# A fused attention and feed-forward kernel on one core: the first weight load ahead of a conversion, two M1 chunks begun in halves, the first M2 part among the M1 chunks

## The chip, the core and the metric

The kernel runs on one core of a Trainium2 chip. The metric is device time in microseconds (us) of one execution. TensorE is called PE, its weight loads PEld, VectorE DVE, ScalarE ACT, GpSimd POOL, and SyncE SP; L577 is line 577 of the kernel before.

## The reference, cut to what matters

Causal attention with a decay per head, then a feed-forward layer on the attention's output. Batch 8, 8 heads, 576 positions, head size 64; so 4608 tokens of 512 numbers, and a hidden layer of 2048.

```python
log_f = np.log(np.clip(f, 0.0001, 1.0));  cum = np.cumsum(log_f, axis=-1)
scores = scale * (q @ k^T) + cum[..., :, None] - cum[..., None, :]   # causal
attn = softmax(scores);  x = attn @ v          # x is then (4608, 512)
h = x @ w_in                                   # "M1" below
out = (h * sigmoid(h)) @ w_out                 # "M2" below
```

## The kernel before, in words

Everything is in bf16 on PE. The order of the instructions on every engine is written out by hand: each engine executes its own list in order, and an instruction waits for the results, buffers or transfers it needs. So a wait on one engine holds everything behind it there.

The tokens are cut into groups g. The first three groups hold the first 128 positions of each batch: g = 0 has batches 0 to 3 (512 columns), g = 1 batches 4 and 5, g = 2 batches 6 and 7 (256 columns each). The rest of each batch comes later, in a loop over 16 pairs of heads.

For the first 128 positions of batch b the steps are `turn0` (L294, PE turns q and k; ACT and DVE copy them out), `scores0` (L328, and the exponential on ACT, L335), for batches 4 to 7 `mask0` (L344, DVE), `out0` (L368, PE; L377 and L383 on DVE), and `back0` (L398, PE turns the output; L399 copies it into x). `convert_v0` (L349) is a POOL instruction that weights v; `out0` needs it.

M1 is cut into chunks (g, fc), 16 chunks to a group. A chunk is four PE matmuls into a PSUM tile `hp` (L577), a tanh on ACT (`th`, L585), and one DVE instruction that makes `gt` (L586) and frees `hp`. M2 works on 128 tokens at a time in four parts of four matmuls each (L622) into one PSUM tile `po`; after the fourth, ACT copies it to `osb` (L632) and SP stores it (L601). There are four `osb` buffers, so the fifth copy waits until the first store has landed. `hp`, `po` and the tiles of `turn0` and `back0` share a PSUM pool of four tiles.

`fill(us)` puts M1 chunks and M2 parts into the list until so many microseconds of PE work are placed; `step(kind)` puts in one of them, kind 1 being an M1 chunk and kind 2 an M2 part; `ready` is the set of groups whose x is there; M2 is first allowed where `open2["w"]` is set. `two_more(b)` handles batches b and b + 1 (b = 4, then 6) with fills in between. `goal` and `spent()` place the later work by the amount of PE work already in the list.

w_in is loaded in four quarters (`load_w_in`, L199) and w_out in four quarters (L203), by transfers that POOL issues and that cast on the way. Chunks fc = 0 to 3 need the first quarter of w_in. POOL also issues the first loads of q, k and v (L132, L141); SP issues the later ones, after it has seen the second quarter of w_out land (`after`, L209). POOL casts the later q and k (L410, L414), SP turns them by a transposing transfer (L437), and PE scores them (L469). Attention on the later positions ends in `attend` (L516 and L525 on PE, L533 and L534 on DVE), and `back` turns the result (L558).

Of the kernel before, what the change touches and what calls it, by code (L numbers as in the profile page):

```python
# [10 lines left out]
FP32 = mybir.dt.float32  # L11
BF16 = mybir.dt.bfloat16
P = 128
# [5 lines left out]
def kernel(  # L19
# [13 lines left out]
    DM, DFF = moe_w_in.shape  # L33
# [29 lines left out]
    tpool = ctx.enter_context(tc.tile_pool(name="tpool", bufs=3))  # L63
# [36 lines left out]
    def xg(g):  # L100
        if g not in xgs:
            tag, bufs = {4 * P: ("x4", 1), 2 * P: ("x2" if g < 3 else "xt", 2), RB: ("x3", 3)}[GW[g]]
            xgs[g] = xpool.tile([P, NCC, GW[g]], BF16, name=tag, tag=tag, bufs=bufs)
        return xgs[g]

    def xcols(g, cc):

        if g == 3 + NM or g == NG - 1:
            x = xg(g)[:, :, :].rearrange("p (u i) t -> p u (i t)", i=2)[:, cc // 2, :]
            return x.rearrange("p (b i s) -> p i b s", i=2, s=ST)[:, cc % 2, :, :]  # L110
        return xg(g)[:, cc, :]
# [85 lines left out]
    def load_w_in(i):  # L197
        c0, c1 = i * DFF // WQ, (i + 1) * DFF // WQ
        nc.gpsimd.dma_start(out=w_in_bf[:, :, c0:c1], in_=w_in_v[:, :, c0:c1])  # L199
# [106 lines left out]
    def ban0(b):  # L306
        sc = psc.tile([P, 2, NP, P], FP32, name="sc", tag="sc")
        for i in range(2):
            nc.tensor.matmul(  # L309
                sc[:, i, :, :].rearrange("p a t -> p (a t)"),  # L310
                lhsT=ident_bf[:, :],
                rhs=ban[:, :, :].rearrange("p a t -> p (a t)"),
                start=True,
                stop=False,
            )
        return sc

    def scores0(b, sc=None):
        t = qT0.pop(b)
        fresh = sc is None  # L320
        u = upool.tile([P, 2, NP, P], BF16, name="u", tag="u")
        u0[b] = u
        if fresh:
            sc = psc.tile([P, 2, NP, P], FP32, name="sc", tag="sc")
        for p in range(NP):
            for i in range(2):
                r = slice(i * D, (i + 1) * D)
                nc.tensor.matmul(  # L328
                    sc[:, i, p, :],
                    lhsT=kT0[b][r, p, :],  # L330
                    rhs=t[r, p, :],
                    start=fresh,
                    stop=fresh or p == NP - 1,
                )
        nc.scalar.activation(  # L335
            out=u[:, :, :, :].rearrange("p i a t -> p (i a t)"),
            in_=sc[:, :, :, :].rearrange("p i a t -> p (i a t)"),
            func=ACT.Exp,
            scale=scale,
        )  # L340
# [7 lines left out]
    def convert_v0(b):  # L348
        nc.gpsimd.tensor_tensor(  # L349
            out=v0[b][:, :, :],  # L350
            in0=vf0.pop(b)[:, :, :],
            in1=w_bf[:, 0, b * H : (b + 1) * H, None].to_broadcast([P, H, D + 1]),
            op=ALU.mult,
        )
# [36 lines left out]
    def back0(b, *copies):  # L391
        xq = xqs.pop(b)[:, :, :].rearrange("p (c j) d -> p c (j d)", j=2)
        g, c0 = HEADS_OF[b]
        k = NCC // len(copies)
        for n, copy in enumerate(copies):
            tx = pbig.tile([P, k, P], BF16, name="tx", tag="big")
            for cc in range(k):
                nc.tensor.transpose(tx[:, cc, :], xq[:, n * k + cc, :], ident_bf[:, :])  # L398
            copy(out=xg(g)[:, n * k : (n + 1) * k, c0 : c0 + P], in_=tx[:, :, :])  # L399
# [167 lines left out]

    gts: dict[int, bass.AP] = {}

    def m1_chunk(g, fc):  # L570
        w = GW[g]
        if fc == 0:
            gts[g] = gpools[g % 3].tile([P, NFC, w], BF16, name="gt", tag=f"gt{g % 3}")
        gt = gts[g]
        hp = pbig.tile([P, w], FP32, name="hp", tag="big")
        for cc in range(NCC):
            nc.tensor.matmul(  # L577
                hp[:, :],
                lhsT=w_in_bf[:, cc, fc * P : (fc + 1) * P],
                rhs=xcols(g, cc),  # L580
                start=(cc == 0),
                stop=(cc == NCC - 1),
            )
        th = tpool.tile([P, w], BF16, name="th", tag="th")
        nc.scalar.activation(out=th[:, :], in_=hp[:, :], func=ACT.Tanh, scale=0.5)  # L585
        nc.vector.scalar_tensor_tensor(  # L586
            out=gt[:, fc, :],
            in0=th[:, :],
            scalar=1.0,
            in1=hp[:, :],  # L590
            op0=ALU.add,
            op1=ALU.mult,
        )
# [88 lines left out]
    at = {"m1": 0, "m2": 0, "left": 0.0}  # L682
# [23 lines left out]
    def step(force=0):  # L706

        a, c = at["m1"], at["m2"]
        want = wanted(a, c)
        if not want:  # L710
            return None
        g1 = M1[a][0] if a < len(M1) else NG
        g2 = M2[c][0] if c < len(M2) else NG
        can1 = g1 in ready and not (M1[a][1] == 0 and g1 > g2 + lag["g"])
        can2 = open2["w"] and c < len(M2) and g2 < g1
        kind = force if (force == 1 and can1) or (force == 2 and can2) else want
        if kind == 1:
            if M1[a][1] == 0:
                begin[g1] = (0, c)
            m1_chunk(g1, M1[a][1])  # L720
            at["m1"] += 1
            t = 4 * (GW[g1] / 2.4 + 2.5)
        else:
            m2_part(*M2[c])
            at["m2"] += 1
            t = 4 * (DM / 2.4 + 2.5)
        return t

    def behind():
        t = sum(4 * (GW[g] / 2.4 + 2.5) for g, _ in M1[at["m1"] :] if g in ready)  # L730
        t += sum(4 * (DM / 2.4 + 2.5) for g, _, _ in M2[at["m2"] :] if g in ready)
        return t / 1000

    def plan(us_):

        a, c, kinds = at["m1"], at["m2"], []
        while us_ > 0:
            k = wanted(a, c)
            if not k:
                break  # L740
            kinds.append(k)
            if k == 1 and M1[a][1] == 0:
                begin[M1[a][0]] = (0, c)
            us_ -= (4 * (GW[M1[a][0]] / 2.4 + 2.5) if k == 1 else 4 * (DM / 2.4 + 2.5)) / 1000
            a, c = a + (k == 1), c + (k == 2)
        return kinds

    def fill(us_, least=0, ends=(0, 0)):

        left = us_ + at["left"]  # L750
        kinds = plan(left)
        kinds += [0] * (least - len(kinds))
        if any(ends) and kinds:
            if 2 not in kinds:
                kinds[0] = 2
            n1, n2 = len(kinds) - kinds.count(2), kinds.count(2)
            e0 = 1 if ends[0] else 0
            e1 = 1 if ends[1] and n2 > e0 else 0
            inner = n2 - e0 - e1
            n = n1 + inner  # L760
            mid = [2 if (x + 1) * inner // n > x * inner // n else 1 for x in range(n)]
            if inner and mid[-1] == 2 and e1 and not e0:
                mid = mid[::-1]
            kinds = [2] * e0 + mid + [2] * e1
        for k in kinds:
            t = step(k)
            if t is None:
                at["left"] = 0.0
                return
            left -= t / 1000  # L770
        at["left"] = left
# [13 lines left out]
    gpool = ctx.enter_context(tc.tile_pool(name="gpool", bufs=1))  # L785
    first_pool = tc.tile_pool(name="first", bufs=1)
    gpools = [first_pool.__enter__(), gpool, gpool]
    convert_v0(0)
    load_w_in(0)
    turn0(1, 0)  # L790
    turn0(1, 1)
    turn0(2, 0)
# [3 lines left out]
    out0(0, apart=True)  # L796
    turn0(3, 0)
    scores0(2, ban0(2))
    convert_v0(2)
    load_w_in(1)  # L800
    turn0(3, 1)
    bans = ban0(3)
    out0(1, apart=True)
# [10 lines left out]
    back0(1, on_act)  # L814
    out0(3, 1)
    back0(2, on_act)
    back0(3, on_act, on_dve)
    ready.add(0)
    nc.gpsimd.memset(trit[0:ST, :], 0.0)
    make_upper_triangular(nc, trit[ST:P, :], val=1.0, diag=True)  # L820
# [36 lines left out]
    def two_more(b):  # L857
        for x in range(2):
            turn0(b + x, 0)
            turn0(b + x, 1)  # L860
        fill(1.2, 2)
        for x in range(2):
            scores0(b + x)
            mask0(b + x)
        fill(2.6 if b == 4 else 3.4, 3)
        out0(b)
        fill(0.6, 1)
        out0(b + 1)
        fill(0.8, 2)
        back0(b, on_act)  # L870
        fill(0.6, 1)
        back0(b + 1, on_act)
        fill(0.6, 1)

    fill(5.9)
    two_more(4)
    ready.add(1)
    fill(3.0)
    open2["w"] = True
    begin[M1[at["m1"]][0]] = (M1[at["m1"]][1], at["m2"])  # L880
    fill(6.0)
    two_more(6)
    ready.add(2)
    fill(4.2)
# [43 lines left out]
    QUAD = [10.9] * (NQ // 2) + [11.7] * (NQ // 2)  # L928

    def spent():  # L930
        t = sum(4 * (GW[g] / 2.4 + 2.5) for g, _ in M1[: at["m1"]])
        return (t + at["m2"] * 4 * (DM / 2.4 + 2.5)) / 1000

    def rest(target):
# [124 lines left out]
```

## Time and profile before

| what | value |
|---|---|
| median of 3 runs | 340.43 us (340.33 to 341.62) |
| the profiled execution: its own time | 340.98 us |
| the profiled execution: span, first to last instruction | 339.2 us |
| PE busy | 330.6 us, 97% |
| ACT busy | 216.9 us, 64% |
| DVE busy | 193.6 us, 57% |
| POOL busy | 137.4 us, 41% |
| granted TensorE clock | 1.0 |

The span is read as a timeline of queues. Busy shares are averages, so what a change in one stretch is worth is read from that stretch: which engine had idle time in it, and what it waited for. A timeline line gives the start, the length, the engine, the line of the kernel, the output and inputs, the count of merged instructions, and in brackets the idle time before it with what ended it. An issue line gives the time from the issue of a transfer to its landing.

### The profile page before, as it was taken

Reading aid. Unit: us, or ns where it says so; the run is one execution under the profiler, and the core shown is the slowest. Engines: PE = TensorE matmul, PEld = TensorE weight load, DVE = VectorE, ACT = ScalarE, POOL = GpSimd, SP = SyncE. Lnnn points to the kernel's source line nnn. Section 1 sums busy time; section 2 is a strip of 40 time slices with the busy share of each in tenths; the row PEclk is TensorE's granted clock in tenths of the full one; section 3 lists DMA queues with packets and bytes.
Section 4 is the critical chain, followed back from the end, with each engine's and each line's share of the span. In section 5 each row is a group of like instructions: output and inputs, shape, how many; then the busy total and the mean of one; then the engine's idle time right before and its main releaser. Section 6 shows DMA issues by size and latency. Waiting matters only on the chain.

```text
span 339.2 us, 10025 instructions
## 1 busy us (share of the span) xinstructions
PE 330.6 (97%) x4132; PEld 222.4 (66%) x4132; DVE 193.6 (57%) x425; ACT 216.9 (64%) x389; POOL 137.4 (41%) x217
## 2 busy tenths in 40 slices
PE   7999899999999999999999999999999999999995
PEld 3745565577656768857766896867776676555654
DVE  4668935267567556655656865684672558334330
ACT  5766635677867767848748784875776485444431
POOL 8895417636756455454374434536060000000000
PEclk9999999999999999999999999999999999999999
DMA  8999999999999799999998969989763210001012
GB/s 151 190 185 222 182 210 155 199 236 177 156 190 236 117 215 134 163 211 151 168 178 172 142 130 175 134 168 165 148 123 66 56 37 33 31 33 64 33 62 63
DMA packets 144702, 48.00 MB, mean 142 GB/s; under 512 B 133328, under 2 KB 139728, under 8 KB 144656
## 3 DMA queue, kind: packets, MB, share of 16 engines
q1 hardware_dynamic: 115088, 36.60, 59.5%
q0 software_dynamic: 29408, 10.62, 26.6%
q8 instruction: 32, 0.52, 0.7%
q10 hardware_dynamic: 160, 0.13, 0.2%
q14 instruction: 14, 0.11, 0.1%
HBM read 36.85 MB, written 9.44 MB: 136 GB/s over the span
## 4 chain that ended last, share of the span: by engine, by line
PE 92%; ACT 2%; DVE 2%; DMA 2%; issue 1%; POOL 0%; POOLq 0%
PE hp L577 35%; PE po L622 24%; PE pr L648 12%; PE sc L469 7%; PE dn L516 6%; PE dn L525 3%; PE tp L294 2%; DMA qkb<-in_k_dram 2%; DVE u L344 1%; DVE gt L586 1%; ACT x L399 1%; PE sc L309 1%; PE sc L328 1%; ACT u L335 1%; PE tx L558 0%
## 5 line engine op out<-in xcount | busy, mean ns | idle before, releaser
L585 ACT ACTIVATE th<-hp 128x384 bf16<-128x384 f32 (+2 forms) x208 | 96.0, 469 | 78.7 <-PE hp L577 75.8
L586 DVE SCALAR_TENSOR_TENSOR gt<-th,hp 128x384 bf16<-128x384 bf16 (+2 forms) x208 | 107.1, 522 | 67.3 <-ACT th L585 58.5
L577 PE MATMUL hp<-x,w_in_bf 128*128 128x384 bf16 (+2 forms) x704 | 122.1, 321 | 1.5 <-ACT x L399 0.9
L577 PEld LDWEIGHTS <-w_in_bf 128*128 128x128 bf16 x832 | 79.4, 98 | 50.6 <-issue 1.8
L622 PE MATMUL po<-w_out_bf,gt 128*128 128x512 bf16 (+1 forms) x400 | 93.8, 371 | 0.0
L480 ACT ACTIVATE u<-sc 128x1024 bf16<-128x1024 f32 (+1 forms) x96 | 74.4, 814 | 6.4 <-PE sc L469 6.4
L622 PEld LDWEIGHTS <-gt 128*128 128x128 bf16 x400 | 37.6, 98 | 32.5 <-issue 0.2
L410 POOL CAST qkb<-qf 128x384 bf16<-128x384 f32 x32 | 16.7, 522 | 95.1 <-DMA qf<-in_q_dram 94.8
L648 PE MATMUL pr<-w_out_bf,gt 64*128 64x256 bf16 x768 | 46.0, 269 | 0.0
L158 POOL DMA_DIRECT2D qkb<-in_k_dram x56 | 43.8, 784 | 0.7 <-issue 0.7
L648 PEld LDWEIGHTS <-gt 64*128 64x128 bf16 x768 | 38.5, 94 | 2.8
L423 POOL TENSOR_TENSOR vp<-vf,w_bf 128x520 bf16<-128x520 f32 (+1 forms) x32 | 34.1, 1069 | 10.3 <-DMA vf<-in_v_dram 9.0
L632 ACT ACTIVATE osb<-po 128x512 f32<-128x512 f32 (+1 forms) x25 | 14.6, 583 | 22.6 <-PE po L622 19.5
L469 PE MATMUL sc<-qkT 64*128 64x128 bf16 (+1 forms) x640 | 27.9, 206 | 0.4 <-ACT u L480 0.3
L469 PEld LDWEIGHTS <-qkT 64*128 64x128 bf16 x640 | 19.9, 94 | 8.6 <-issue 6.5
L486 DVE TENSOR_TENSOR u<-u,tri 128x768 bf16<-128x768 bf16 x32 | 19.4, 605 | 10.5 <-ACT u L480 10.5
L474 ACT ACTIVATE ut<-sc 128x640 bf16<-128x640 f32 x32 | 22.5, 702 | 1.7 <-PE sc L469 1.3
L516 PEld LDWEIGHTS <-u 128*128 128x128 bf16 x576 | 20.6, 98 | 2.9
L516 PE MATMUL dn<-vp,u 128*128 128x65 bf16 x384 | 21.8, 194 | 0.0
L534 DVE TENSOR_TENSOR xr<-dn,rec 128x448 bf16<-128x448 f32 x32 | 20.0, 624 | 1.1
L516 PE MATMUL dn<-v,u 128*128 128x65 bf16 x192 | 20.0, 194 | 0.0
L577 PE MATMUL hp<-xt,w_in_bf 128*128 128x256 bf16 x128 | 16.6, 273 | 0.0
(72 smaller groups left out, 228.1 us busy)
## 6 DMA issues: line engine op xcount, KB each, us to landing
out_dram<-osb SPq DMA_DIRECT2D x32, 256.0 KB, 3.5
vf<-in_v_dram SPq DMA_DIRECT2D x26, 256.0 KB, 5.5
qf<-in_q_dram SPq DMA_DIRECT2D x64, 96.0 KB, 3.4
qkb<-in_k_dram POOLq DMA_DIRECT2D x56, 48.0 KB, 4.6
w_in_bf<-in_moe_w_in_dram POOLq DMA_DIRECT2D x4, 512.0 KB, 6.8
w_out_bf<-in_moe_w_out_dram POOLq DMA_DIRECT2D x4, 512.0 KB, 8.7
vf<-in_v_dram POOLq DMA_DIRECT2D x6, 256.0 KB, 10.3
qkb<-in_q_dram POOLq DMA_DIRECT2D x8, 128.0 KB, 5.5
```

Of the source, the lines that this page charges most:

```text
L158: nc.gpsimd.dma_start(out=t2[:, NR + 1 : NX, j * D : (j + 1) * D], in_=k[b, head(p, j), P:SM, :].rearrange("(c p) d -> p c d", p=P),)
L423: nc.gpsimd.tensor_tensor(out=vbf[b][r, c, :, :], in0=vst[b][c][r, :, :], in1=w_bf[r, c + 1, b * H : (b + 1) * H, None].to_broadcast([n, H ...
L469: nc.tensor.matmul(sc[:, i, o : o + q1 - q0], lhsT=kt, rhs=t[r, q0:q1], start=True, stop=True)
L474: nc.scalar.activation(out=ut[:, :, 0:3:2, :].rearrange("p k i t -> p i k t"), in_=sc[:, :, T0 : T0 + (NM + 1) * ST].rearrange("p i (k t) ...
L480: nc.scalar.activation(out=u[:, :, c * SM : c * SM + w], in_=sc[:, :, 0:w], func=ACT.Exp, scale=scale)
L516: nc.tensor.matmul(dn[:, i * NR + c - 1, :], lhsT=u[:, i, o : o + P], rhs=vals(kb, i), start=(kb == 0), stop=(kb == c),)
L534: nc.vector.tensor_tensor(out=xq[:, :, p % 2, :], in0=dn[:, :, 0:D], in1=rec[:, :, None].to_broadcast([P, NGR, D]), op=ALU.mult,)
L577: nc.tensor.matmul(hp[:, :], lhsT=w_in_bf[:, cc, fc * P : (fc + 1) * P], rhs=xcols(g, cc), start=(cc == 0), stop=(cc == NCC - 1),)
L585: nc.scalar.activation(out=th[:, :], in_=hp[:, :], func=ACT.Tanh, scale=0.5)
L586: nc.vector.scalar_tensor_tensor(out=gt[:, fc, :], in0=th[:, :], scalar=1.0, in1=hp[:, :], op0=ALU.add, op1=ALU.mult,)
L622: nc.tensor.matmul(po[:, :], lhsT=gt[:, fc, tb * P : (tb + 1) * P], rhs=w_out_bf[:, fc, m0:m1], start=(fc == 0), stop=(fc == NFC - 1),)
L648: nc.tensor.matmul(pos[g, tb][y], lhsT=gt[r, fc, tb * P : (tb + 1) * P], rhs=w_out_bf[r, fc, y * DM // 2 : (y + 1) * DM // 2], start=(half ...
```

## The change

Three things are moved, and the amount of arithmetic stays the same.

1. On POOL's list the load of the first quarter of w_in stands ahead of `convert_v0(0)` instead of behind it, and that of the second quarter ahead of `convert_v0(2)`.
2. Chunks (0, 0) and (0, 1) are each cut into two halves of 256 columns. The halves for batches 0 and 1 are put on PE's list around the last `back0`, one before it and one after it, and their tanh and DVE instructions behind it. The other halves come where the whole chunks were.
3. At the end of `two_more(4)` an M2 part stands in place of a `fill` that found nothing to place, and the M1 chunks of g = 1 that follow are mixed with M2 parts from the start instead of seven chunks ahead of the first part.

By the lists of the two kernels, PE has eight matmuls more (840 of L577 instead of 832), ACT two more tanh and DVE two more `gt` instructions. Some M1 chunks and M2 parts change places up to the fourth of the 16 blocks of the loop; from its attention on, PE's list is the same.

```diff
+    EARLY = 2
+    def cols(g, fc):
+        return slice(2 * P if g == 0 and fc < EARLY else 0, GW[g])
+    def m1_cost(g, fc):
+        r = cols(g, fc)
+        return 4 * ((r.stop - r.start) / 2.4 + 2.5)
     def m1_chunk(g, fc):
+        m1_gate(*m1_mm(g, fc, cols(g, fc)))
+    def m1_mm(g, fc, r):
...
-        hp = pbig.tile([P, w], FP32, name="hp", tag="big")
+        hp = pbig.tile([P, r.stop - r.start], FP32, name="hp", tag="big")
...
-                rhs=xcols(g, cc),
+                rhs=xcols(g, cc) if whole_ else xg(g)[:, cc, r],
...
+    def m1_gate(g, fc, r, hp):
...
+    load_w_in(0)
     convert_v0(0)
-    load_w_in(0)
...
+    load_w_in(1)
     convert_v0(2)
-    load_w_in(1)
...
     back0(2, on_act)
+    first = [m1_mm(0, 0, slice(0, 2 * P))]
     back0(3, on_act, on_dve)
+    first.append(m1_mm(0, 1, slice(0, 2 * P)))
+    for x in first:
+        m1_gate(*x)
...
         back0(b + 1, on_act)
-        fill(0.6, 1)
-
-    fill(5.9)
+        if b == 4:
+            open2["w"] = True
+            step(2)
+        else:
+            fill(0.6, 1)
+
+    fill(5.0)
     two_more(4)
     ready.add(1)
-    fill(3.0)
-    open2["w"] = True
+    for kind in (1, 1, 2, 1, 1, 2, 1, 1, 1, 2):
+        assert step(kind) is not None
+    at["left"] = 0.0
     begin[M1[at["m1"]][0]] = (M1[at["m1"]][1], at["m2"])
-    fill(6.0)
+    fill(2.6)
     two_more(6)
```

More of the change, by code (lines that the diff above doesn't have):

```diff
@@ L568 @@
     gts: dict[int, bass.AP] = {}
+    EARLY = 2
[4 more added lines that the diff above has]
+        return 4 * ((r.stop - r.start) / 2.4 + 2.5)
     def m1_chunk(g, fc):
+        m1_gate(*m1_mm(g, fc, cols(g, fc)))
+    def m1_mm(g, fc, r):
         w = GW[g]
-        if fc == 0:
+        if g not in gts:
             gts[g] = gpools[g % 3].tile([P, NFC, w], BF16, name="gt", tag=f"gt{g % 3}")
-        gt = gts[g]
-        hp = pbig.tile([P, w], FP32, name="hp", tag="big")
+        hp = pbig.tile([P, r.stop - r.start], FP32, name="hp", tag="big")
+        whole_ = r.start == 0 and r.stop == w
         for cc in range(NCC):
@@ L583, in m1_chunk @@
             )
-        th = tpool.tile([P, w], BF16, name="th", tag="th")
+        return g, fc, r, hp
+    def m1_gate(g, fc, r, hp):
+        th = tpool.tile([P, r.stop - r.start], BF16, name="th", tag="th")
         nc.scalar.activation(out=th[:, :], in_=hp[:, :], func=ACT.Tanh, scale=0.5)
         nc.vector.scalar_tensor_tensor(
-            out=gt[:, fc, :],
+            out=gts[g][:, fc, r],
             in0=th[:, :],
@@ L721, in step @@
             at["m1"] += 1
-            t = 4 * (GW[g1] / 2.4 + 2.5)
+            t = m1_cost(*M1[a])
         else:
@@ L729, in behind @@
     def behind():
-        t = sum(4 * (GW[g] / 2.4 + 2.5) for g, _ in M1[at["m1"] :] if g in ready)
+        t = sum(m1_cost(g, fc) for g, fc in M1[at["m1"] :] if g in ready)
         t += sum(4 * (DM / 2.4 + 2.5) for g, _, _ in M2[at["m2"] :] if g in ready)
@@ L743, in plan @@
                 begin[M1[a][0]] = (0, c)
-            us_ -= (4 * (GW[M1[a][0]] / 2.4 + 2.5) if k == 1 else 4 * (DM / 2.4 + 2.5)) / 1000
+            us_ -= (m1_cost(*M1[a]) if k == 1 else 4 * (DM / 2.4 + 2.5)) / 1000
             a, c = a + (k == 1), c + (k == 2)
@@ L930, in spent @@
     def spent():
-        t = sum(4 * (GW[g] / 2.4 + 2.5) for g, _ in M1[: at["m1"]])
+        t = sum(m1_cost(g, fc) for g, fc in M1[: at["m1"]])
         return (t + at["m2"] * 4 * (DM / 2.4 + 2.5)) / 1000
```

## The prediction

> **What bounds the kernel now.** I read the page first, then busy time by stretch.
>
> ```profile
> span 339.2 us, 10025 instructions
> PE 330.6 (97%) x4132; PEld 222.4 (66%) x4132; DVE 193.6 (57%) x425; ACT 216.9 (64%) x389; POOL 137.4 (41%) x217
> ...
> PE 92%; ACT 2%; DVE 2%; DMA 2%; issue 1%; POOL 0%; POOLq 0%
> ```
>
> PE carries 92% of the chain that ended last, so only PE's idle time can be won.
>
> ```profile
> 18.40:38.00 19.60, 18.34 (x168) 9.18 (x168) 15.68 (x24) 12.87 (x23) 15.19 (x25) 1.00 1.18 199
> 38.00:48.00 10.00, 9.58 (x64) 6.15 (x63) 5.02 (x12) 4.68 (x12) 0.00 (x0) 1.00 1.19 205
> 48.00:64.00 16.00, 16.00 (x184) 9.95 (x184) 7.30 (x14) 8.20 (x16) 10.73 (x15) 1.00 1.16 178
> 64.00:85.00 21.00, 20.75 (x308) 14.40 (x307) 12.79 (x33) 16.88 (x32) 11.57 (x19) 1.00 1.30 201
> ```
>
> The columns are the stretch, its length, the busy time of PE, PEld, DVE, ACT and POOL, the clock, the DMA share, GB/s. From 38.4 to 310 us PE is idle for well under 1 us in all. So whatever PE is ahead by when the mixed M1 and M2 work starts stays to the end, unless it meets a new wait. The tail after 310 us is left as it is. PE's timeline shows the idle time before that point:
>
> ```profile
> 17.72 0.61 PE L398 MATMUL tx<-ident_bf,xq 128*128 128x128 bf16 x4 [0.30 <-DVE xq L383]
> 18.46 6.20 PE L577 MATMUL hp<-x,w_in_bf 128*128 128x512 bf16 x28
> ...
> 36.23 1.02 PE L577 MATMUL hp<-x,w_in_bf 128*128 128x512 bf16 x4 [0.19 <-DVE gt L586]
> 37.09 0.39 PE L398 MATMUL tx<-ident_bf,xq 128*128 128x128 bf16 x4
> 38.42 3.22 PE L577 MATMUL hp<-x,w_in_bf 128*128 128x256 bf16 x28 [0.94 <-ACT x L399]
> ```
>
> PE waits around 18 us for the attention of batch 3 and its copies, then in small pieces from 33 us for DVE, then 0.94 us for the copy of batch 5. DVE is late there because its two masks collide with POOL's conversions (the next two lines, from the timelines of DVE and POOL):
>
> ```profile
> 29.99 2.96 DVE L344 TENSOR_TENSOR u<-u,tri 128x1024 bf16<-128x1024 bf16 x2 [0.22 <-ACT u L335]
> 29.89 2.51 POOL L349 TENSOR_TENSOR v<-vf,w_bf 128x520 bf16<-128x520 f32 x2 [4.04 <-DMA vf<-in_v_dram]
> ```
>
> At 52.86 us the same two masks take 1.85 us.
>
> **The early halves.** The half of chunk (0, 0) needs the copies of batches 0 and 1; ACT ends the second at 17.44. PE's turn of batch 2 is out at 17.4, so the half starts at 17.49. The matmul spacing from the rows: (6.20 - 0.38)/27 = 0.216 us for 512 columns, (3.22 - 0.27)/27 = 0.109 us for 256. So the half takes 0.44 us, to 17.92. Batch 3's turn follows at 17.92 to 18.19 (before 17.72 to 18.28 with its waits), the second half at 18.19 to 18.62; its `hp` tile waits for ACT's copy of batch 2, at 18.04. ACT's last copy ends 0.2 us later, at 18.61; the other halves run 18.66 to 19.53; five whole chunks of 0.863 us end at 23.85. Before, seven chunks from 18.46 ended at 24.51: PE is 0.66 us earlier. Eight pairs of 256 columns instead of eight of 512 cost 8 x (0.218 - 0.216), nothing. Two more tanh (0.38 us each) and `gt` (0.42 us) cost nothing: ACT idles 0.27 us before each tanh here and DVE 0.17 us before each `gt`. If that cover fails, `hp` tiles come free late and up to 0.66 us is lost. Bounds: 0 to 0.75.
>
> The Trainium skill ("TensorE: Matmul & The Clock Gate", "Back-to-back issue gap") speaks against the split: it gives a sustained 81 ns per matmul of 128 columns and 131 ns of 512, so by an estimate between them a pair of 256 would cost some 65 ns more than one of 512, 0.5 us over eight pairs. By that rule the gain at the end would be some 0.6 us instead of the sum below. The spacings of 216 and 109 ns in this trace do not agree with it, and I keep the trace's.
>
> **The loads.** w_in's first quarter landed 5.7 us after its issue at 11.28, at 17.0, in time for 17.49 even unmoved. On POOL the load fits between the end of the v issues (9.38) and `convert_v0(0)` (10.28, which waits for the weights), so no conversion moves by over 0.1 us, and `convert_v0(3)` still waits for its v (issued 8.45, landed about 14.7). What moves is the transfers:
>
> ```profile
> 11.00:12.00 1.00, 1.00 (x35) 0.80 (x30) 0.80 (x2) 0.70 (x2) 1.00 (x2) 1.00 1.17 282
> 12.00:13.00 1.00, 1.00 (x25) 0.67 (x21) 0.93 (x5) 1.00 (x2) 0.98 (x2) 1.00 0.61 126
> 13.00:14.00 1.00, 1.00 (x26) 0.65 (x24) 0.34 (x1) 0.77 (x2) 1.00 (x2) 1.00 0.73 65
> 14.00:15.00 1.00, 1.00 (x18) 0.56 (x12) 0.74 (x2) 0.71 (x1) 0.98 (x3) 1.00 1.23 204
> ```
>
> The DMA share is 1.2 when full, and 0.61 and 0.73 from 12 to 14 us: 0.9 us of idle transfer time, which w_in, issued 1.9 us earlier, fills. Later landings queue behind it (10.2 us from issue for v of batch 4), so all come some 1.0 us earlier, between 0 and 1.5.
>
> **DVE's chain to the first chunk of g = 1.** Exponentials come 0.66 us earlier with PE (29.3 and 30.2), and the conversions of batches 4 and 5 about 1.0 us earlier (28.9 and 29.9). In the trace each mask ended 0.55 us after the conversion it met. So the masks end at about 30.5 and 31.95 instead of 32.95: 1.0 us earlier, between 0.65 (PE's lead alone) and 1.45 (no collision, 0.92 us each). The rest is DVE's list as before: three `gt`, the output of batch 4 (34.6), `gt`, output of batch 5 (36.0). PE turns batch 5 at 36.1, ACT copies it by 37.4 instead of 38.38.
>
> **The M2 part.** The wait for that copy is now covered by four matmuls of L622 (0.86 us). Their PSUM tile is that of chunk (0, 13), freed by DVE behind the output of batch 5, at 36.62, so they run 36.67 to 37.53 and the first chunk of g = 1 starts at 37.53, 0.89 us earlier than 38.42 with 0.86 us more done: 1.75 us ahead (bounds 1.4 to 2.2). w_out's quarters landed at 33.3, 35.9, 38.4 and 41.5, even unmoved before the four parts of the first tile are due (36.7, 38.4, 40.1 and 42.3, from 0.86 us a part and 0.44 a chunk). The tile that `po` holds leaves three for the chunks; the order puts at most three between parts.
>
> **Where part of it is given back.** PE's list has the fifth finished M2 tile further ahead: before, its last part and an M1 chunk stood behind both attentions of the first block; now they stand ahead of them. Its copy to `osb` waits for the first store to land, and in the new list the tile of the second attention waits for that copy. ACT and SP before:
>
> ```profile
> 73.19 0.60 ACT L632 ACTIVATE osb<-po 128x512 f32<-128x512 f32 x1 [0.48 <-PE po L622]
> 66.70 2.38 SPq L601 DMA_DIRECT2D out_dram<-osb  x4
> out_dram<-osb SPq DMA_DIRECT2D x1, 256.0 KB, 3.4
> ```
>
> The first store landed at 66.70 + 3.4 = 70.1, 3 us before it was needed. Now ACT reaches the copy at about 69.0. SP's list there follows POOL casts and transfers, so it moves with the transfers: landing at 69.1, copy to 69.75. PE starts the first attention at 69.98 - 1.75 + 0.88 (work moved ahead of it) = 69.1, the second at 70.06 with no wait. But ACT's next two tanh, two `gt` and then both attentions' outputs follow on DVE: `gt` to 70.8, output 1 to 71.6, output 2 to 72.45, and PE, with only 0.55 us of scores between, waits 0.9 us to turn it at 72.5. Before, with the same work done, it did so at 73.63. PE is then 1.1 us ahead: 0.6 us are given back, because nothing stands any more between the second attention and its turn. Bounds: 1.5 ahead with no wait at ACT, 0.1 ahead if the store lands unmoved at 70.1.
>
> Later waits have cover: the transposed q and k of block 2's second pair landed 1.7 us before use, before, and PE's list has 0.9 us more ahead of it now; the others landed over 5 us early.
>
> **Sum.** 1.75 - 0.6 = 1.1 us. The profiled execution would go from 340.98 to 339.9; the median of the runs shown is 0.55 below it, so I predict 340.43 - 1.1 = 339.3.
>
> **Rivals.**
>
> *All of it passes.* The store lands well before ACT needs it (the transfers gain 1.5 us), DVE follows at once, the masks collide less: 1.6 to 2.3 us ahead, about 338.5. For it: transfers are saturated up to 110 us. Against: the output chain of DVE alone takes 1.1 us, with 0.55 us of PE work over it. Chance 0.22.
>
> *Nothing is left.* The transfers do not move, since w_in only waits behind v of batch 3, which landed at 14.7 anyway. Then the store lands at 70.1 and PE turns at 73.55: 340.3, between 339.9 and 340.7. Chance 0.15.
>
> *Slower through the first store.* SP's loads now begin while the last w_out quarters still flow, and the store meets a full queue. A v load between 81 and 90 us took 6.8 us to land; the median of v loads is 5.5. A store of 5.5 us instead of 3.4, issued at 65.7 to 66.7, lands at 71.2 to 72.2; ACT stands still with the exponentials behind it, and the turn is at 74.6 to 75.6: 1.0 to 2.0 us slower than before, about 341.8. It decides where the store lands after 70.2; each later microsecond costs one. Chance 0.16, a good third of it beyond 0.5%.
>
> *The halves do not start early* (an `hp` tile or the w_in quarter late): 0.66 us less at 24 us, but DVE's collision and the M2 part stay, so 0.5 us ahead, 339.9. It lies in the forecast's own range.
>
> **Numbers.** The forecast (0.5 to 1.6 us ahead, 338.8 to 339.9) has 0.47. 0.5% is 1.7 us, about what a measurement of this kernel can tell from no change. Faster by more: most of the first rival, 0.2. Slower by more: 0.06. The rest, 0.74, within. The range takes in the first rival, the second and the start of the third: 338.2 to 341.0.
>
> **What would show it.** In the changed profile: L577 with 256 columns at 17.5; the DMA share full from 12 to 14 us; the two masks of L344 ending near 32 us; four matmuls of L622 ahead of the first chunk of g = 1, that chunk near 37.5; a wait of ACT's copy L632 for a store near 69 us and of PE's L558 for DVE near 72 us; no new wait behind it. I am wrong if PE is not ahead at 38 us, or if the lead at 38 us is lost or kept whole at 73 us.

## The result: 1% slower, and the profile after

The changed kernel takes 345.76 us (median of twelve runs, 341.0 to 347.3) beside 340.75 us for the kernel before on the same chip (twelve runs, 340.3 to 341.69): a ratio of 1.0104, 95% interval 1.0071 to 1.0137. The profiled execution took 345.63 us, with a span of 343.9. (Here and below a ratio leaves out executions that took over 1.5% more than the fastest of their kernel, here five of the twelve, so it is below the quotient of the two medians, 1.0147.)

The page of the changed kernel: span, PE's busy time, and its chain of waits. PE is busy for 1.4 us less than before in a span that is 4.7 us longer (some of it because records are missing: PE shows 4109 matmuls for 4140 weight loads), and DMA, 2% of the chain before, is 10% of it now.

```profile
span 343.9 us, 10017 instructions
PE 329.2 (96%) x4109; PEld 224.3 (65%) x4140; DVE 193.8 (56%) x427; ACT 217.4 (63%) x391; POOL 138.4 (40%) x217
...
PE 82%; DMA 10%; POOL 2%; issue 2%; DVE 1%; ACT 1%; ACTq 0%; POOLq 0%
```

Busy time by stretch, with the columns as before. The last stretch says where to look: PE is idle for 4.4 us of 21 there (0.25 before), and the granted clock is 0.92 instead of 1.00.

```profile
18.40:38.00 19.60, 19.20 (x183) 10.80 (x185) 15.72 (x27) 13.67 (x25) 15.21 (x25) 1.00 1.14 187
38.00:48.00 10.00, 9.40 (x103) 6.35 (x103) 4.15 (x10) 4.63 (x11) 0.18 (x1) 1.00 1.20 207
48.00:64.00 16.00, 15.74 (x149) 9.65 (x147) 7.51 (x15) 9.16 (x17) 9.41 (x14) 1.00 0.94 167
64.00:85.00 21.00, 16.62 (x219) 11.30 (x221) 9.77 (x24) 13.57 (x27) 13.09 (x21) 0.92 1.28 217
```

PE's timeline, up to the first chunk of g = 1 and the one long wait behind it. The half-chunk waits 0.97 us for w_in and starts at 17.87, not at the 17.49 of the prediction; the M2 part (L638 now, L622 before) and the first chunk of g = 1 (L590, before L577) come at 36.60 and 37.46, where 36.67 and 37.53 were expected. The last row is a wait that the prediction had ruled out: the fourth M2 part of the first tile stands for 0.55 us, because w_out's last quarter lands at 42.92 and not at 41.49 as in the profile of before.

```profile
17.87 0.61 PE L590 MATMUL hp<-x,w_in_bf 128*128 128x256 bf16 x4 [0.97 <-DMA w_in_bf<-in_moe_w_in_dram]
...
36.60 1.02 PE L638 MATMUL po<-w_out_bf,gt 128*128 128x512 bf16 x4
37.46 1.04 PE L590 MATMUL hp<-x,w_in_bf 128*128 128x256 bf16 x8
...
42.96 1.89 PE L638 MATMUL po<-w_out_bf,gt 128*128 128x512 bf16 x7 [0.55 <-DMA w_out_bf<-in_moe_w_out_dram]
```

The two masks of batches 4 and 5 on DVE end at 31.88 (predicted 31.95, before 32.95). Beside them is POOL's pair of conversions, which starts 0.2 us later than before, not 1.0 us earlier.

```profile
29.73 0.69 DVE L344 TENSOR_TENSOR u<-u,tri 128x1024 bf16<-128x1024 bf16 x1 [0.23 <-ACT u L335]
30.64 1.24 DVE L344 TENSOR_TENSOR u<-u,tri 128x1024 bf16<-128x1024 bf16 x1 [0.22 <-ACT u L335]
```

```profile
30.10 2.69 POOL L349 TENSOR_TENSOR v<-vf,w_bf 128x520 bf16<-128x520 f32 x2 [3.84 <-DMA vf<-in_v_dram]
```

So PE was ahead at 38 us as forecast, measured against the one profile of before. Then ACT's fifth `osb` copy (L648, before L632), SP's first store, and the store's time from issue to landing:

```profile
72.67 0.60 ACT L648 ACTIVATE osb<-po 128x512 f32<-128x512 f32 x1 [3.21 <-DMA out_dram<-osb]
```

```profile
68.29 2.70 SPq L617 DMA_DIRECT2D out_dram<-osb  x4
```

```profile
out_dram<-osb SPq DMA_DIRECT2D x1, 256.0 KB, 4.3
```

The store is issued 1.6 us later than before and flies 0.9 us longer, so it lands at 72.59 and not at the 69.1 of the prediction. ACT stands for 3.2 us, and PE for 2.9 us ahead of the second attention, whose `dn` tile waits for the copy. PE's timeline there (lines between left out):

```profile
73.32 0.19 PE L516 MATMUL dn<-v,u 128*128 128x65 bf16 x1 [2.90 <-ACT osb L648]
...
75.93 0.93 PE L558 MATMUL tx<-ident_bf,xr 128*128 128x128 bf16 x7 [1.04 <-DVE xr L534]
77.08 1.49 PE L638 MATMUL po<-w_out_bf,gt 128*128 128x512 bf16 x3 [0.22 <-issue]
```

The last two rows have a second loss in them. The group of seven turns takes 0.93 us, and 0.56 us in the kernel with five `osb` tiles below. The granted clock, microsecond by microsecond (the third number from the end of a row), says why:

```profile
75.00:76.00 1.00, 0.07 (x1) 0.07 (x2) 0.84 (x3) 1.00 (x2) 0.00 (x0) 0.88 1.30 276
76.00:77.00 1.00, 0.86 (x7) 0.80 (x9) 0.10 (x1) 0.65 (x1) 0.70 (x3) 0.50 1.13 359
77.00:78.00 1.00, 0.92 (x3) 0.37 (x3) 0.58 (x2) 0.00 (x0) 1.00 (x3) 0.50 1.01 228
78.00:79.00 1.00, 1.00 (x6) 0.54 (x4) 0.00 (x0) 0.00 (x0) 0.54 (x2) 0.50 0.87 184
79.00:80.00 1.00, 1.00 (x10) 0.84 (x8) 0.19 (x1) 0.55 (x2) 1.00 (x3) 0.92 1.44 170
```

If the clock is either 1.0 or 0.5, it was 0.5 for 0.24 + 3 + 0.16 = 3.4 us.

### The profile page after: what moved, and what is told of

Its sections match the earlier page's. It is cut to its first block, busy times and chain, and to the rows that moved or that the text cites. A ratio compares the mean times of both kernels' runs of the same rounds, so it can differ in the third digit from the quotient of the medians.

```text
span 343.9 us, 10017 instructions
## 1 busy us (share of the span) xinstructions
PE 329.2 (96%) x4109; PEld 224.3 (65%) x4140; DVE 193.8 (56%) x427; ACT 217.4 (63%) x391; POOL 138.4 (40%) x217
## 3 DMA queue, kind: packets, MB, share of 16 engines
q1 hardware_dynamic: 115088, 36.60, 57.1%
## 4 chain that ended last, share of the span: by engine, by line
PE 82%; DMA 10%; POOL 2%; issue 2%; DVE 1%; ACT 1%; ACTq 0%; POOLq 0%
PE hp L590 30%; PE po L638 23%; PE pr L664 12%; PE sc L469 7%; PE dn L516 5%; DMA vf<-in_v_dram 5%; DMA w_out_bf<-in_moe_w_out_dram 3%; PE dn L525 3%; DMA qkb<-in_k_dram 1%; DMA out_dram<-osb 1%; DVE gt L602 1%; POOL v L349 1%; PE tp L294 1%; POOL qkb L132 1%; PE tx L558 1%
## 5 line engine op out<-in xcount | busy, mean ns | idle before, releaser
L590 PE MATMUL hp<-x,w_in_bf 128*128 128x384 bf16 (+2 forms) x709 | 122.7, 320 | 1.2 <-DMA w_in_bf<-in_moe_w_in_dram 1.0
L590 PEld LDWEIGHTS <-w_in_bf 128*128 128x128 bf16 x840 | 80.3, 98 | 50.3 <-DMA w_in_bf<-in_moe_w_in_dram 1.1
L638 PE MATMUL po<-w_out_bf,gt 128*128 128x512 bf16 (+1 forms) x373 | 90.2, 372 | 2.6 <-issue 0.7
L638 PEld LDWEIGHTS <-gt 128*128 128x128 bf16 x400 | 37.8, 98 | 33.0 <-issue 1.7
L648 ACT ACTIVATE osb<-po 128x512 f32<-128x512 f32 (+1 forms) x25 | 14.6, 583 | 24.9 <-PE po L638 21.7
L486 DVE TENSOR_TENSOR u<-u,tri 128x768 bf16<-128x768 bf16 x32 | 20.5, 641 | 10.8 <-ACT u L480 10.8
L590 PE MATMUL hp<-xt,w_in_bf 128*128 128x256 bf16 x128 | 16.6, 273 | 0.0
```

What stands on the lines that cost most here:

```text
L486: nc.vector.tensor_tensor(out=x, in0=x, in1=tri[:, None, None, :].to_broadcast([P, 2, NR, P]), op=ALU.mult)
L590: nc.tensor.matmul(hp[:, :], lhsT=w_in_bf[:, cc, fc * P : (fc + 1) * P], rhs=xcols(g, cc) if whole_ else xg(g)[:, cc, r], start=(cc == 0), ...
L638: nc.tensor.matmul(po[:, :], lhsT=gt[:, fc, tb * P : (tb + 1) * P], rhs=w_out_bf[:, fc, m0:m1], start=(fc == 0), stop=(fc == NFC - 1),)
```

## The experiments

Theories at the start. *Store*: the loss is the place of the fifth `osb` copy, which in the new list is reached before the first store lands. *Loads*: the moved w_in loads delay the whole stream of transfers, whatever waits for it. Later came *clock*: part of the loss is the half clock that follows PE's idle time.

To compare traces I use PE's **lead** over the profile of before: at the last matmul of an attention, how much earlier it is, plus the M1 and M2 work that is done beyond that of before (at the spacings of the rows: 0.216, 0.163 and 0.109 us for 512, 384 and 256 columns). The table has all kernels, with the store's issue and landing.

| kernel | median, us | ratio to before (95%) | store issued, landed | lead at end of attention 2, 4, 8, 32 |
|---|---|---|---|---|
| changed | 345.76 | 1.0104 (1.0071 to 1.0137) | 68.29, 72.59 | -1.62, -4.17, -4.66, -4.66 |
| e1_five_osb | 340.79 | 1.0005 (0.9990 to 1.0021) | 65.81, 68.95 | 1.87, 1.13, -0.11, -0.39 |
| e2_old_loads | 344.86 | 1.0105 (1.0072 to 1.0139) | 67.76, 72.54 | -1.57, -5.46, -5.95, -5.99 |
| e3_loads_alone | 340.89 | 1.0009 (0.9990 to 1.0028) | 68.69, 73.78 | 0.30, -0.29, -0.31, -0.31 |
| e4_m2_alone | 345.39 | 1.0085 (1.0050 to 1.0119) | 68.61, 73.87 | -3.26, -4.46, -5.02, -5.02 |
| e5_halves_alone | 340.38 | 0.9977 (0.9954 to 1.0000) | 65.76, 69.26 | 0.50, 0.43, 0.43, 0.37 |
| e8_store_early | 340.68 | 0.9986 (0.9969 to 1.0003) | 65.14, 68.10 | 1.41, 0.68, 0.19, 0.20 |
| e9_dummy | 344.77 | 1.0097 (1.0071 to 1.0122) | 67.88, 72.64 | -1.67, -2.66, -3.81, -4.16 |
| e10_part_behind | 339.55 | 0.9951 (0.9932 to 0.9969) | 67.67, 71.91 | 1.45, 1.51, 1.05, 1.27 |
| e11_behind_old_loads | 339.49 | 0.9955 (0.9938 to 0.9973) | 68.09, 72.39 | 1.03, 1.08, 0.98, 0.51 |
| e12_behind_five_osb | 339.21 | 0.9949 (0.9931 to 0.9966) | 65.48, 68.65 | 1.78, 1.84, 1.89, 2.20 |
| e13_m2_alone_behind | 340.48 | 0.9985 (0.9963 to 1.0006) | 68.17, 73.51 | 1.17, 0.95, 0.00, 0.26 |
| e7_before_five_osb | 340.36 | 0.9985 (0.9965 to 1.0005) | 68.20, 73.28 | 1.02, 1.13, 0.30, 0.30 |

A lead comes from one execution each. e7 has PE's list of before, and its lead of 1.0 at 72 us is what two executions of nearly the same list can differ by; differences under 1 us are read from the ratios, or from averages over the profiles.

### e1_five_osb: no wait for a store

```diff
-    opool = ctx.enter_context(tc.tile_pool(name="opool", bufs=4))
+    opool = ctx.enter_context(tc.tile_pool(name="opool", bufs=5))
...
-    ban = const.tile([P, NP, P], BF16, name="ban")
-    warm = const.tile([P, SM], BF16, name="warm")
+    ban = w_out_bf[:, 1, :].rearrange("p (a t) -> p a t", t=P)
+    warm = w_out_bf[:, 0, :]
```

> The changed kernel with a fifth osb tile, so that ACT's fifth copy waits for no store (the room for it comes from warm and ban, which lie in rows of w_out_bf that are loaded later). Store theory (the loss is that this copy, placed ahead of the second attention, waits for the first store to land): no 3.2 us wait ahead of L648, PE idle for less than 1.2 us in 64 to 85 us instead of 4.4, the clock there 1.00, and the time at 339.3 to 340.5. Load theory (the reordered loads delay everything, whatever waits for them): the wait moves to another place, the time stays at 343 to 346.

The wait is gone, the clock stays at 1.00, and with it the loss: 340.79 us. So the store theory holds. (It is the twelve times that show it: in this one profile the store landed at 68.95, just as ACT's copy began at 68.92, so here four tiles would hardly have waited either.) But the time is that of before, not 1 us better, although PE's lead at the second attention is 1.87 us. Of that, 0.74 goes at the turn, which waits for DVE's outputs as predicted, and 1.24 more by 109 us:

```profile
103.61 2.77 PE L590 MATMUL hp<-x,w_in_bf 128*128 128x384 bf16 x16
107.49 0.19 PE L516 MATMUL dn<-v,u 128*128 128x65 bf16 x1 [1.11 <-DVE gt L602]
```

```profile
104.50 1.01 DVE L492 TENSOR_TENSOR ut<-ut,trit 128x128 bf16<-128x128 bf16 x1
105.43 0.55 DVE L486 TENSOR_TENSOR u<-u,tri 128x768 bf16<-128x768 bf16 x1
105.90 1.07 DVE L492 TENSOR_TENSOR ut<-ut,trit 128x128 bf16<-128x128 bf16 x1
106.89 1.93 DVE L602 SCALAR_TENSOR_TENSOR gt<-th,hp 128x384 bf16<-128x384 bf16 x4
```

These are PE's and DVE's timelines. Sixteen matmuls in a row are four M1 chunks, so all four PSUM tiles of that pool hold an `hp`, and the attention's `dn` needs the first one back. DVE frees it behind the masks, and the two of L492, 0.22 us in the median of their line, take 1.0 us each; POOL issues two loads from 103.99 to 105.57 and converts v from 105.59 to 108.01 beside them. PE's list is the changed kernel's own: before, there is an M2 part and then three chunks at this place. That these four chunks are the cause is read from the rows; no run changes them alone.

### e2_old_loads: the changed kernel without its moved loads

```diff
-    load_w_in(0)
     convert_v0(0)
+    load_w_in(0)
...
-    load_w_in(1)
     convert_v0(2)
+    load_w_in(1)
```

> The changed kernel with the two w_in loads behind the conversions again, as before the change; early halves and M2 parts as changed. Load theory: all landings come back to those of before (w_out's last quarter 41.5 instead of 42.9), the first store is issued at 66.7 instead of 68.3 and lands near 70.1, the wait of ACT's copy L648 falls from 3.2 us to 1 or less: 340.0 to 341.0. Store theory without a part for the loads: the store still lands near 72, the wait stays at 2.5 to 3.5 us, 344 to 346.

The same loss, the same ratio, and a store that lands at 72.54. The loads are not the cause.

### e3_loads_alone: the kernel before with its loads moved

```diff
+    load_w_in(0)
     convert_v0(0)
-    load_w_in(0)
...
+    load_w_in(1)
     convert_v0(2)
-    load_w_in(1)
```

> The kernel before with only the two w_in loads moved ahead of the conversions. Load theory: landings 0.5 to 1.9 us later than before, as in the changed kernel, PE waits for them or for what follows from them, 342 to 345. Store theory: the landings may be as late, but the copy L632 that needs the first store stands 4 us later in ACT's list, so the store is still in time (lands by 72.6, needed at 73.2): 340.3 to 341.0. My prediction's step on the loads, if it holds alone: landings 1.0 us earlier, 339.6 to 340.3.

No difference from before. The landings are late here too (w_out's last quarter 43.77 instead of 41.49), but over all fourteen profiles the place of the loads makes no difference to that: w_in's first quarter lands at 17.43 on average in the seven kernels with moved loads and at 17.11 in the seven without, w_out's last at 42.29 and 42.40. The store lands at 73.78 here, 0.6 us behind the 73.2 at which the old list reaches the copy, and the lead falls from 0.30 to -0.29: a microsecond for a microsecond.

### e4_m2_alone: the M2 parts and the written order alone

```diff
-        fill(0.6, 1)
+        if b == 4:
+            open2["w"] = True
+            step(2)
+        else:
+            fill(0.6, 1)
...
-    fill(3.0)
-    open2["w"] = True
+    for kind in (1, 1, 2, 1, 1, 2, 1, 1, 1, 2):
+        assert step(kind) is not None
+    at["left"] = 0.0
...
-    fill(6.0)
+    fill(2.6)
```

> The kernel before with only the M2 parts moved ahead and the written order of ten steps; no early halves, loads as before. Store theory: ACT reaches the fifth copy L632 near 69.7 and waits for the first store (70.1 in the profile of before, up to 72.6 in that of the changed kernel): a wait of 0.5 to 3 us, 340.0 to 344. Load theory: no loss, since the loads are unmoved: 339.3 to 340.3. What tells them apart besides the time is the idle time of PE from 64 to 76 us: over 1.5 us by the store theory, under 0.6 us by the other.

The loss is here in full. ACT's copy waits longest of all, and PE is idle for 4.1 us between 64 and 76 us:

```profile
73.95 0.60 ACT L632 ACTIVATE osb<-po 128x512 f32<-128x512 f32 x1 [4.32 <-DMA out_dram<-osb]
```

### e5_halves_alone: the early halves alone

The functions that cut a chunk are in it as in the change; the lines that use them:

```diff
...
     back0(2, on_act)
+    first = [m1_mm(0, 0, slice(0, 2 * P))]
     back0(3, on_act, on_dve)
+    first.append(m1_mm(0, 1, slice(0, 2 * P)))
+    for x in first:
+        m1_gate(*x)
...
-    fill(5.9)
+    fill(5.0)
```

> The kernel before with only the early halves of the first two M1 chunks; loads and M2 parts as before. Store theory: the fifth osb copy stands where it stood before, needed near 73, so no loss: 340.0 to 341.0; my prediction's step alone gives PE 0.66 us ahead by 24 us and 0.5 at the end, 340.2. If the halves themselves cost (more matmuls of 256 columns, PSUM tiles held longer), PE is behind at 24 us and the time is 341.5 or more.

The lead is 0.5 us and stays, and the ratio is 0.9977 (0.9954 to 1.0000). The halves do no harm; the loss is all in the M2 part's edit.

### e8_store_early: the same list, the store sooner

```diff
     fill(4.2)
+    store(1)
```

> The changed kernel with the first store alone issued earlier on SP, ahead of the loads and the transposes of block 0's last pair instead of behind them. Store theory: it is issued near 65.3 us instead of 68.3, lands by 69.7, ACT's fifth copy waits for under 0.7 us, PE's clock stays at 1.00, and the time is 340.0 to 341.5. If what holds the second attention is not the store but the DMA stream in general, the wait turns up at the transposes that are now 0.7 us later, 343 or more.

SP issues the store at 65.14 and it lands at 68.10. ACT copies at 69.37 without a wait:

```profile
65.14 0.57 SPq L617 DMA_DIRECT2D out_dram<-osb  x1
```

```profile
69.37 0.62 ACT L648 ACTIVATE osb<-po 128x512 f32<-128x512 f32 x1
```

The loss is gone a second way, with ACT's and PE's lists as changed. As in e1, the lead shrinks to nearly nothing by 109 us.

### e9_dummy: PE kept busy while it waits

```diff
         attend(n)
+        if m == 0:
+            t = psc.tile([P, 2, SM], FP32, name="sc", tag="sc")
+            for _ in range(12):
+                nc.tensor.matmul(t[:, 0, :], lhsT=warm[:, 0:P], rhs=warm[:, :], start=True, stop=True)
         attend(n + 1)
```

> The changed kernel with twelve extra matmuls of zeros (2.6 us) on PE between the two attentions of the first block, into a PSUM tile of the scores that is free there; they compute nothing that is used. Clock theory (part of the loss is the half clock that PE is granted for 3.4 or 6.8 us after it stood idle for some 3 us): the wait for the store stays, the clock stays at 1.00, and the time falls by 1.5 to 2.5 us to 343.0 to 344.3. If the half clock costs nothing (PE waits anyway in those microseconds) or does not come from the idle time: 345 to 346, as the changed kernel.

The wait stays (the copy comes at 72.72), and the clock stays at 1.00. PE's timeline, then two of the microseconds that stood at 0.50 above:

```profile
69.69 2.75 PE L1045 MATMUL sc<-warm 128*128 128x512 bf16 x12
```

```profile
76.00:77.00 1.00, 1.00 (x10) 0.67 (x11) 0.42 (x1) 0.70 (x1) 0.68 (x2) 1.00 1.11 356
77.00:78.00 1.00, 1.00 (x9) 0.78 (x8) 0.27 (x2) 0.12 (x1) 1.00 (x3) 1.00 0.92 205
```

Between attentions 2 and 4 the changed kernel loses 2.55 us of lead, this one 0.99: by these two profiles the half clock costs 1.56 us. In the median 1.0 us comes back, less than expected; in the profiles this kernel then loses 1.15 us near 109 us and the changed kernel, later there, only 0.49. The two ratios, 1.0097 and 1.0104, are not told apart, so the price of the clock rests on the profiles. The runs of the changed kernel go the same way, though in them a longer wait and a lower clock come together. Its three runs with a mean granted clock of 0.998 or more took 341.0, 343.6 and 344.3 us, its six at 0.994 or 0.995 took 345.4 to 346.6, and its three at 0.990 took 345.1 to 347.3.

The Trainium skill ("TensorE: Matmul & The Clock Gate", "HAM oscillation — how this bites in real kernels") warns of idle gaps of PE over some 3.4 us, and gives half clock as the state that follows. The trace agrees on the half clock and on the step of 3.4 us. It differs on the gap: 2.90 us idle and 1.04 us more a little later were enough in the changed kernel, while 0.92 and 1.04 us in e9 were not.

### e10_part_behind: the fifth tile's last part back behind the attentions

```diff
     two_more(6)
     ready.add(2)
-    fill(4.2)
+    fill(3.8)
```

> The changed kernel with the last stretch of work ahead of block 0 planned at 3.8 us instead of 4.2, so that the fifth M2 tile's last part falls behind both attentions again, as before the change; loads and halves stay changed. Store theory: ACT's copy is needed near 72.5 us and waits for a store that lands at 70 to 74, hidden or nearly: PE idle for under 1.5 us in 64 to 76 us, 339.8 to 341.3. If the earlier M2 parts cost in another way than by the place of this copy: 343 or more.

By the lists of the two kernels the edit moves more than this part: on PE's list the part now stands behind the turn of the first block as well, and M1 chunks and M2 parts stand about one place later as far as the end of the loop. 339.55 us: 0.5% below the kernel before, with the buffers of before. The store lands late, at 71.91, but the copy comes only at 73.04 and waits for no store:

```profile
73.04 0.60 ACT L648 ACTIVATE osb<-po 128x512 f32<-128x512 f32 x1
```

The four chunks in a row are gone as well; at that place PE's timeline has an M2 part and two chunks, and no wait ahead of the attention:

```profile
103.50 1.04 PE L638 MATMUL po<-w_out_bf,gt 128*128 128x512 bf16 x4
104.38 1.46 PE L590 MATMUL hp<-x,w_in_bf 128*128 128x384 bf16 x8
105.68 0.19 PE L516 MATMUL dn<-v,u 128*128 128x65 bf16 x1
```

### The last four, around e10

e11_behind_old_loads is e10 with the loads where they were:

```diff
-    load_w_in(0)
     convert_v0(0)
+    load_w_in(0)
...
-    load_w_in(1)
     convert_v0(2)
+    load_w_in(1)
```

> The kernel of e10_part_behind (fifth M2 tile's last part behind both attentions) with the w_in loads behind the conversions again. If the moved loads do nothing: the same time as e10, 339.0 to 340.1 beside a kernel before of 340.7. If they hold w_in's first quarter back or bring the stream forward by 1 us, as my prediction had it: 0.5 to 1.0 us away from e10.

339.49 us: the moved loads do nothing, good or bad.

e12_behind_five_osb is e10 with the fifth `osb` tile of e1 (the room for it made as there):

```diff
-    opool = ctx.enter_context(tc.tile_pool(name="opool", bufs=4))
+    opool = ctx.enter_context(tc.tile_pool(name="opool", bufs=5))
```

> The kernel of e10_part_behind with the fifth osb tile of e1_five_osb. Order theory (with five osb tiles the changed kernel lost its lead of 1.9 us between 72 and 111 us because of the order of its list there, four M1 chunks in a row ahead of an attention): with the order of e10 the lead stays at 1.0 us or more behind 111 us, 339.0 to 340.0. Supply theory (whatever lead PE has, it runs into what DMA and POOL deliver near 107 us): the lead is gone there as in e1, 340.3 to 341.0.

The lead stays: 1.89 us behind 109 us, where e1 with the other order had lost all of it. So it was the order and not the supply that ate the lead in e1; here w_out's last quarter landed at 40.53 us, there at 40.99. At 339.21 us (0.9949) it is the lowest median, not told apart from e10.

e13_m2_alone_behind is e4 with the last part behind, so e10 without the halves and with the old loads:

```diff
-    fill(4.2)
+    fill(3.8)
```

> The kernel before with the M2 parts moved ahead and the last part of the fifth tile behind both attentions (as e10_part_behind), but without early halves and with the loads as before. By my prediction's steps the M2 part in the old wait is worth 0.9 us at 38 us and the halves 0.5 of the rest: this should end some 0.4 us above e10, 339.5 to 340.4. If the halves are worth nothing behind the M2 part: as e10, 339.0 to 339.9.

340.48 us, 0.9 us above e10 instead of 0.4. Its lead goes from 0.95 to 0.00 between attentions 4 and 5, at a wait of 0.8 us for transposed q and k that landed at 86.28. In the profile of before they landed at 84.53: this is the supply wait that the prediction thought covered, met in an execution whose transfers run late (w_out's last quarter landed at 42.75).

e7_before_five_osb is the kernel before with the fifth tile alone (again with that room):

```diff
-    opool = ctx.enter_context(tc.tile_pool(name="opool", bufs=4))
+    opool = ctx.enter_context(tc.tile_pool(name="opool", bufs=5))
```

> The kernel before with the fifth osb tile alone (warm and ban moved into rows of w_out_bf). Store theory: in the order of before the store is awaited only when it lands behind 73.2 us, so the fifth tile saves 0 to 0.6 us: 340.0 to 340.8. If more osb tiles help in general, later too (stores in the way all along the kernel): under 339.7.

340.36 us, not told apart from before. The fifth tile is worth something only where the list needs it early.

## Why the prediction was wrong, step by step

**The early halves: the right kind, too large.** The lead at 24 us was 0.26 us (PE's turn of batch 4 at 24.34 instead of 24.60), not 0.66. "In time for 17.49 even unmoved" was read from one landing at 17.0; in fourteen profiles w_in's first quarter lands between 16.6 and 17.8, and in seven of the nine profiles with halves the first half waits for it. That is the rival "the halves do not start early", which held in part. Alone they gave a lead of 0.5 us (e5). Averages say the same as the one pair of profiles: batch 4's turn comes at 24.03 us in the nine profiles with halves and at 24.29 in the five without. The extra cost that the Trainium skill ("TensorE: Matmul & The Clock Gate", "Back-to-back issue gap") would give the halves, 65 ns a pair by the prediction's estimate, is not in the trace: with 0.27 us for the last, the row at 17.87 has (0.61 - 0.27)/3 = 0.113 us a matmul, so 0.226 for a pair beside 0.216 for one of 512 columns.

**The loads: wrong.** The DMA share between 12 and 14 us rose, from 0.61 and 0.73 to 0.84 and 1.28, and nothing landed earlier for it. v of batch 3 landed at 14.85 (14.67 before) and w_in's first quarter behind it at 17.83 (16.94 before). The argument of the rival "nothing is left", that w_in waits behind v of batch 3 in any case, fits this.

**DVE's chain: right number, by luck.** The masks ended within 0.1 us of the forecast. But e7, with loads and list as before, ends them at 31.70 and e13 at 31.61. So the prediction wanted to win back a collision that was in good part that one execution's, and the conversions, which were to come 1.0 us earlier, came 0.2 us later.

**The M2 part: right in kind, at the low end in size.** It started 0.07 us from the forecast, and without the store's wait the lead at the second attention is 1.87 us (e1) and 1.41 us (e8), where 1.75 was forecast at 38 us. But the profile of before was late there: e7, with the same list, starts the first chunk of g = 1 at 37.16 and not at 38.42. On average that chunk comes at 37.28 in the ten profiles with the moved M2 part and at 37.83 in the four without, which with the part's 0.86 us makes 1.4 us, the lower bound of the forecast. And w_out's last quarter, "even unmoved before" the fourth part, landed 0.5 us behind its need.

**"Given back": the step that failed.** The chain on DVE was right: where the store does not hold it, PE's turn L558 comes at 72.19 (e1) and 72.64 (e8), with 72.5 forecast. Its price was not: the 73.63 of before is not "with the same work done". Only the M2 part moved ahead; the M1 chunk beside it (0.44 us) stood ahead of that turn before and stands behind it now. So 72.5 is 0.7 us ahead and not 1.1, and the leads of e1 and e8 at attention 4 are 1.13 and 0.68. What turned the gain into a loss is the store's landing, which was wrong by 3.5 us, 72.59 for 69.1. The issue was put at 65.7, from 66.70 in the profile of before less 1.0 for the loads; it was 68.29. In the thirteen profiles with SP's old order (all but e8) the issue stands 24.2 to 25.6 us behind the landing of w_out's last quarter, and that landing varies from 40.53 to 43.77; the 41.49 of the profile of before was one of the early ones. The flight was put at 3.4 us and was 4.3: it is 3.0 to 3.5 us in the five profiles where the store is issued before 67 us, and 4.2 to 5.3 in the nine where it is issued later. In the old list, which needs the copy at 73.2, that spread is nearly hidden; the changed list reaches the copy at 69.5 and shows it in full.

**The sum.** Forecast 1.1 us ahead, measured 4.66 behind, 5.76 us apart in the profiles. The store: 3.43 (L558 at 75.93 instead of 72.5). The M1 chunk that the prediction took as done there: 0.44. PE is then 75.93 - 73.63 + 0.44 = 2.74 us behind, and 4.17 at attention 4: 1.43 more, about what the half clock costs (1.56 beside e9). Near 109 us, where the four chunks stand in a row: 0.49. The last two were in no step. "Whatever PE is ahead by stays to the end" left out that idle time of PE lowers its clock, and that PE's list differed as far as the fourth block.

**The rivals.** "Slower through the first store" had the mechanism, the place and the rule that each later microsecond costs one. Its price of 1.0 to 2.0 us was too low, by a landing up to 72.2 and without the clock, and its chance of 0.16 rested on the store of a single profile. The chance of a loss over 0.5% was put at 0.06.

What stays open: why the transfers up to 43 us vary by 3 us from one execution to the next, and why a store issued after 67 us flies 1 to 2 us longer. e8 says only that it goes with the moment of issue or the place in SP's queue: in a stream as late as the changed kernel's (w_out's last quarter at 42.95) the early store still took 2.96 us. Open too is which part of the order costs the lead near 109 us, since e10 and e12 change it at many places at once.

## What to carry to other kernels

When a change brings a buffer's user forward, price the buffer's release by its spread over executions, not by one profile: a release 3 us ahead of its need hides that spread, and a need moved 4 us forward shows it all. A long idle gap of the matmul engine can cost more than its length: here three gaps of 2.9 to 4.0 us were followed by 3.4 to 6.8 us at half clock. And a change that does harm may not have to go as a whole: planning 0.4 us less work ahead of the first attentions, which puts the last part of the fifth M2 tile behind them again, turned a loss of 1% into a gain of 0.5%.

## What the runs showed of the hardware

Half clock was granted in steps: 3.4 us in the changed kernel and in e4, twice that in e2, each time beginning 0.4 to 2.4 us after PE had resumed from a gap of 2.9 to 4.0 us. The first store, 256 KB in all kernels, took from 2.96 us (e8) to 5.34 us (e13) to land.
